# Sums of w_out by accumulating transfers: four whole ones, the last two issued behind the low words of w_in

## The chip, the cores and the metric

The kernel runs on one core of one Trainium2 chip. The metric is the device time of an execution in microseconds, as the median of several runs.

## What is computed

The reference first runs a chunked state-space block over `x`, `a`, `B` and `C` (batch 4, 8 heads, 768 tokens, 32 channels a head, 16 states), then brings its output into the shape 3072 tokens by 256 channels, and runs a two-layer block on it:

```
x = attn_out.transpose(0, 2, 1, 3).reshape(3072, 256)
h = x @ w_in                                  # 256 x 2048
g = where(h > 0, h, exp(min(h, 0)) - 1)       # ELU
out = g @ w_out                               # 2048 x 256
```

All inputs and the output are float32 (the two weights come in 64 bits and are brought to float32 on the chip).

## The kernel before

The tokens are cut into 12 blocks of 256 (`BLK`), numbered `n`. For each block the scan (scores, decays, states) makes its rows `y`, the first layer makes 2048 hidden values in tiles of 128 features, and the second layer multiplies them with `w_out`. The order of all instructions on all engines is written out by hand; there is no planner. An engine works off its own instructions in this order, and waits for semaphores where another engine or a transfer has to be done first. GpSimd and ScalarE also issue transfers, and these stand in the same order as their other work.

The first blocks take both layers directly (`l1`, `l2`). From block 2 on, blocks go in pairs:

- First layer, `l1_words(n, m)`: activations and weights are split into a high and a low word, and three passes of products fill two PSUM tiles, `ps_h` and `ps_w`. Then ScalarE scales `ps_w` into `e` (L796), VectorE joins it to `ps_h` (L799), ScalarE makes the exponential (L805, L806 in `begin_end`), and VectorE writes the hidden values `g` (L813 in `end_words`). The weights' words come from `words_of_w(p)` (ScalarE L737 and VectorE L738) and `low_of_w(p)` (two GpSimd subtractions, by `sub`, L848), for eight pieces `p` of `w_in`.
- Second layer, `second(n)`: a seven-product scheme over two blocks and two halves of `w_out`. It needs four blocks of `w_out`, called `a11, a12, a21, a22` here (`a_out[0]`, `[1]`, `[2]`, `[3]`), and four sums of them: `s3 = a11 - a21`, `s2 = a22 - s3`, `s4 = a12 - s2`, and `s1 = a21 + a22`. `s2, s3, s4` are tiles of their own (`s_out[0]`, `[1]`, `[2]`); `s1` is written over `a21`, so `a_out[2]` holds it from then on. Products are taken in the order r = 0 to 6 with the weights `(a11, a12, s1, s2, s3, a22, s4)`, first for four of the eight feature pairs `i` (half 0), then for the other four. GpSimd supplies differences of the hidden values: `sum_t1`, `sum_t2`, and the subtractions behind r = 0 and r = 1.

The sums of `w_out` are made by two helpers. `less` is a ScalarE instruction (L711) that writes the negative of one block into a sum's tile. `plus` (L715) is a transfer, issued by GpSimd, that adds one block to what stands at its destination. A whole block is 8 pieces of 128 by 128 for all partitions, 512 KB.

Around the change the order is this. The loop over `j` from 8 to 15 (`i = j - 8`) runs the first layer of block pair 2 with `l1_words(2, j)`, and puts in between the words of `w_in`, the second layer of block 1 by `l2(1, 0)` to `l2(1, 7)`, which reads all of the unchanged `w_out` (its last two steps at `i == 7`), and the scan of blocks 4 and 5. Behind the loop come `end_words()`, the low words of pieces 1 and 2, transfers, the words of piece 3, `decay(6, 0)`, the low words of piece 3, `sum_t2(2, 0)` (four subtractions) and one more subtraction on GpSimd. Then the loop over `n = 4, 6, 8, 10` begins: sixteen steps `k`, each an `l1_words(n, k)` of 6 products and some steps of `second(n - 2)`, four products for r = 0 in the first step and three steps or so a step after that. `turn_step` puts the scan's next operands in between, among them `mask_heads` (L465, the tile `ctm`) on VectorE. The text calls the way from the `j` loop into `n = 4` the first border.

In `second`, the products at r = 2 are the first that read `s1`, and those at r = 6 the first that read `s4`. The tile for r = 0, 2, 4, 6 of half 0 comes from a pool with one buffer, so r = 2 begins only when r = 0's tile was copied away to `p_sum` (L919, ScalarE).

Of the kernel before, what the change touches and what calls it, by code (L numbers as in the profile page):

```python
# [14 lines left out]
ALU = mybir.AluOpType  # L15
# [17 lines left out]
def kernel(  # L33
# [27 lines left out]
    nc = tc.nc  # L61
# [30 lines left out]
    for k in range(4):  # L92
        (nc.scalar if k % 2 else nc.sync).dma_start(
            out=la0[BH * k:BH * (k + 1)],
            in_=a.rearrange("b h (c s) -> (b h) c s", s=P)[:, 0:2, :])
# [25 lines left out]
    def load_bc(n, c_queue=nc.sync, us=(0, 1)):  # L121
        b, g = place(n)
        if "bc" not in st.setdefault(n, {}):
            st[n]["bc"] = raw.tile([P, 2, 2, NH, N], F32, tag="bc", name="bc", bufs=2)
        if n > 3:
            for k in range(2):
                load_squares(n, k)
            return
        for u in us:
            sl = slice((2 * g + u) * P, (2 * g + u + 1) * P)  # L130
            for k, src in enumerate((B,) if n == 1 else (B, C)):
                (nc.sync, c_queue)[k].dma_start(
                    out=st[n]["bc"][:, k, u], in_=src[b, :, sl, :].rearrange("h s n -> s h n"))

    def load_b(n):
        b, g = place(n)
        st.setdefault(n, {})["b"] = raw.tile([P, 2, NH, N], F32, tag="b", name="b_tok", bufs=2)
        for u in range(2):
            sl = slice((2 * g + u) * P, (2 * g + u + 1) * P)
            nc.sync.dma_start(  # L140
                out=st[n]["b"][:, u], in_=B[b, :, sl, :].rearrange("h s n -> s h n"))
# [141 lines left out]
    for v in range(2):  # L283
        nc.gpsimd.affine_select(
            out=low16[Q * v:Q * v + Q], in_=low16[Q * v:Q * v + Q], pattern=[[1, Q]],
# [5 lines left out]
        out=hmask, in_=hmask, pattern=[[-N, NH]], compare_op=ALU.is_ge, fill=0.0,  # L291
        base=0, channel_multiplier=1)
    nc.gpsimd.affine_select(
        out=hmask, in_=hmask, pattern=[[N, NH]], compare_op=ALU.is_ge, fill=0.0,
# [8 lines left out]
        out=minus, in0=ident, scalar1=-1.0, scalar2=None, op0=ALU.mult)  # L303
# [102 lines left out]
    def scaled(n, eng):  # L406

        s = st[n]
        s["sc"] = sc = s["b"] if n > 3 else raw.tile(
            [P, 2, NH, N], F32, tag="b", name="sc", bufs=2)  # L410
        factor = eb0[:, :, NH * n:NH * (n + 1)] if n < 2 else eb[:, :, rows_of(n)]
        eng.tensor_tensor(
            out=sc, in0=s["b"] if n > 3 else s["bc"][:, 0],
            in1=factor.unsqueeze(3).to_broadcast([P, 2, NH, N]), op=ALU.mult)
# [54 lines left out]
    def turn_part(n, part):  # L469
        if part < 2:  # L470
            turn_square(n, 1 - part)
        elif part == 2:
            mask_heads(n)
        else:
            turn_exp(n)
# [233 lines left out]
    def less(out, in_):  # L709

        nc.scalar.activation(out, in_, ACT.Copy, scale=-1.0)  # L711

    def plus(out, in_, rows=slice(None)):

        nc.gpsimd.dma_start(out=out[:, rows], in_=in_[:, rows], accum_op=ALU.add)  # L715

    def weight_sums():
        return [conv.tile([P, MC // 2, P], F32, tag="w64", name="w_sum", bufs=W_AHEAD)
# [3 lines left out]
    a_out = [w_parts[:, k, r] for r in range(2) for k in range(2)]  # L722
    s_out = []
# [8 lines left out]
    def words_of_w(i):  # L732

        w = pieces[i][0]
        k_words[i] = conv.tile(
            [P, 2, KC, CW], F32R, tag="w64", name="w_words", bufs=W_AHEAD)
        nc.scalar.activation(k_words[i][:, 0], w, ACT.Copy, scale=NEAR)  # L737
        nc.vector.scalar_tensor_tensor(  # L738
            out=k_words[i][:, 1], in0=k_words[i][:, 0].bitcast(F32), scalar=1.0 / WORD - 1.0,
            in1=w, op0=ALU.mult, op1=ALU.add)  # L740

    def low_of_w(i):

        w0 = conv.tile([P, KC, CW], F32R, tag="w_in", name="w0", bufs=DF // CW + 1)
        for k in range(KC):
            sub(w0[:, k], pieces[i][0][:, k], k_words[i][:, 0, k].bitcast(F32))
        k_words[i] = k_words[i], w0
# [30 lines left out]
    def l1_words(n, m, between=None):  # L778

        cols = slice(m % 2 * P, (m % 2 + 1) * P)  # L780
        w, w0 = k_words[m // 2]
        w1, both_w, w0 = w[:, 0, :, cols], w[:, 1, :, cols], w0[:, :, cols]
        y1, y0, both_y = y_words[n]
        high, both = psum([P, 2 * BLK], "ps_h"), psum([P, 2 * BLK], "ps_w")
        passes = [(high, w1, y1), (high, w0, y0), (both, both_w, both_y)]
        for ps, lhs, rhs in passes if m == (8 if n == 2 else 0) or m == 15 else passes[2:] + passes[:2]:
            for k in range(KC):
                nc.tensor.matmul(  # L788
                    out=ps, lhsT=lhs[:, k], rhs=rhs[:, k], start=k == 0 and lhs is not w0,
                    stop=k == KC - 1 and lhs is not w1)  # L790
        if between:
            words_of_y(between)
            if between == 4:
                both_of_y(4)
        e = ffn.tile([P, 2 * BLK], F32, tag="e", name="e", bufs=2)
        nc.scalar.activation(e, both, ACT.Copy, scale=WORD)  # L796
        if late:
            end_words()
        nc.vector.scalar_tensor_tensor(  # L799
            out=high, in0=high, scalar=WORD - 1.0, in1=e, op0=ALU.mult, op1=ALU.add)  # L800
        late.append((n, m, high, e))

    def begin_end():
        high, e = late[-1][2:]
        nc.scalar.activation(e, high, ACT.Relu, scale=-1.0)  # L805
        nc.scalar.activation(e, e, ACT.Exp, scale=-1.0)  # L806
# [12 lines left out]
    def row_of(n):  # L819
        b, g = place(n)  # L820
        return b * S + g * BLK
# [3 lines left out]
    def l2(n, j, half=None):  # L825


        if j == 0 and half != 1:
            o_of[n] = p_o.tile([P, 2, DM], F32, tag="o", name="ps_o")
        for m in (2 * j, 2 * j + 1) if half is None else (2 * j + half,):  # L830
            for ts in range(2):
                nc.tensor.matmul(  # L832
                    out=o_of[n][:, ts], lhsT=g_of[n, j][:, m % 2, ts * P:(ts + 1) * P],
                    rhs=w_out[:, m], start=(m == 0 and ts == 0), stop=(m == MC - 1),
                    skip_group_check=True)
        if j == MC // 2 - 1 and half != 0:
            ob = ffn.tile([P, 2, DM], F32, tag="tmp", name="ob", bufs=1)
            nc.scalar.copy(out=ob, in_=o_of.pop(n))
            r0 = row_of(n)
            nc.sync.dma_start(  # L840
                out=out[r0:r0 + BLK, :].rearrange("(t p) e -> p t e", p=P), in_=ob)
# [5 lines left out]
    def sub(out, in0, in1):  # L847
        nc.gpsimd.tensor_tensor(out=out, in0=in0, in1=in1, op=ALU.subtract)  # L848
# [291 lines left out]
    def weigh_two(m, q):  # L1140
        weigh(m, q)
        weigh(m + 1, q)
# [29 lines left out]
    for j in range(2 * DIRECT):  # L1172
        n, i = 2 + j // DIRECT, j % DIRECT
# [53 lines left out]
    for j in range(8, 16):  # L1227
        i = j - 8
        l1_words(2, j, between=4 if i == 7 else None)
        for p in ((), (6,), (), (7,), (0,), (1,), (2,), ())[i]:  # L1230
            words_of_w(p)
        for p in ((), (), (6,), (7,), (0,), (), (), ())[i]:
            low_of_w(p)
        if i == 7:
            l2(1, 6)
            l2(1, 7)
        begin_end()
        if i == 0:
            turn_part(5, 2)
            scaled(4, nc.gpsimd)  # L1240
            scaled(5, nc.gpsimd)
        if i < 2:
            load_bc(i + 6)
            l2(1, i)
        if i == 2:
            l2(1, 2, half=0)
            scores(4, 5)
            sums(4, 5)
            for q in range(4):
                weigh_two(4, q)  # L1250
            l2(1, 2, half=1)
            states(4)
            states(5)
            turn_part(4, 3)
            turn_part(5, 3)
            for to in (6, 7):
                load_b(to)
                spread_cum(to)
        if i == 3:
            l2(1, 3)  # L1260
        if i == 4:
            y = across(4, 5)
            inside(y, 4, 5, ts=(0,))
            l2(1, 4)
        if i == 5:
            l2(1, 5, half=0)
            inside(y, 4, 5, ts=(1,))
            l2(1, 5, half=1)
        if i in (0, 1, 3, 4):
            sum_t1(2, (0, 1, 3, 4).index(i))  # L1270
        if i in (4, 6):
            turn_part(6, i // 2 - 2)
        if i == 2:
            less(s_out[0], s_out[1])
            plus(s_out[0], a_out[3])
        if i == 5:
            plus(a_out[2], a_out[3], slice(0, 4))
    end_words()
    less(s_out[2], s_out[0])
    for p in (1, 2):  # L1280
        low_of_w(p)
    plus(s_out[2], a_out[1])
    plus(a_out[2], a_out[3], slice(4, 8))
    words_of_w(3)
    decay(6, 0)
    low_of_w(3)
# [102 lines left out]
```

## Time and profile before

| | |
|---|---|
| median of 3 runs | 355.28 us (354.91 to 355.96) |
| profiled execution | 354.39 us |
| its span, first to last instruction | 352.7 us |
| mean granted TensorE clock | 0.99 |
| PE busy | 342.7 us, 97% of the span |
| DVE (VectorE) busy | 258.6 us, 73% |
| ACT (ScalarE) busy | 238.2 us, 68% |
| POOL (GpSimd) busy | 214.9 us, 61% |
| accumulating transfers | 5 issues on GpSimd: 3 of 512 KB, 2 of 256 KB |

In the views, PE is TensorE's products and PEld its weight loads. A row of a timeline has the start and the length in us from the start of the span, the engine, the line of the kernel, the operation, what it writes and reads with the shape, and how many were merged into the row; a bracket at the end is idle time of that engine just before, and what ended it. A row of the stretches has the stretch, its length, the busy time of PE, PEld, DVE, ACT and POOL with their counts, the granted TensorE clock as a share of full speed, the busy share of the DMA engines and GB/s. GpSimd's rows can overlap, because an instruction is recorded from when it is taken up.

### The profile page before, as it was taken

The numbers are of one execution on the slowest core, as the hardware profiler recorded it, in microseconds if no ns is written. First come the engines' busy times: TensorE is split into PE (matmuls) and PEld (weight loads), VectorE is DVE, ScalarE is ACT, GpSimd is POOL, SyncE is SP. The second block draws the span as 40 slices with busy tenths as digits, with TensorE's granted clock in tenths as the row PEclk, the third lists the DMA queues.
The fourth block names the chain that finished last, engine by engine and source line by source line (L and its number), as shares of the span: only waits on it lengthen the run. The fifth ranks groups of instructions, "written<-read, shape, count | busy, mean of one in ns | idle before, by whom it ended". The sixth has DMA issues, their size and how long they took to land.

```text
span 352.7 us, 9862 instructions
## 1 busy us (share of the span) xinstructions
PE 342.7 (97%) x3878; PEld 299.9 (85%) x3878; DVE 258.6 (73%) x504; ACT 238.2 (68%) x541; POOL 214.9 (61%) x321
## 2 busy tenths in 40 slices
PE   8999999999999869999999999999999999999996
PEld 5669888888787759988989988899988999999996
DVE  3898979979889677784978685878685757565232
ACT  5789988798766858837599737599646666655000
POOL 5654564569896695975176964086954074455760
PEclk9999999999999978999999999999999999999999
DMA  8977988473693940052150062140000100001001
GB/s 144 253 200 175 309 196 209 89 127 64 102 187 47 171 62 30 4 92 78 52 113 30 2 113 58 61 74 3 0 2 4 62 0 3 0 0 46 17 1 60
DMA packets 76902, 28.58 MB, mean 81 GB/s; under 512 B 57848, under 2 KB 71736, under 8 KB 76856
## 3 DMA queue, kind: packets, MB, share of 16 engines
q1 hardware_dynamic: 70360, 25.60, 31.1%
q0 software_dynamic: 4176, 2.10, 5.4%
q8 instruction: 30, 0.49, 0.6%
q10 hardware_dynamic: 2320, 0.26, 0.5%
q14 instruction: 16, 0.13, 0.1%
HBM read 22.51 MB, written 3.34 MB: 73 GB/s over the span
## 4 chain that ended last, share of the span: by engine, by line
PE 82%; DVE 7%; ACT 3%; issue 3%; SPq 2%; DMA 2%; POOL 0%; DVEq 0%; POOLq 0%; ACTq 0%
PE ps_o L907 34%; PE ps_h L788 17%; PE ps_h L671 11%; PE ps_w L788 8%; PE ps_o L832 5%; PE ps_y L638 2%; PE ps_g L545 2%; DMA w<-in_moe_w_in_dram 2%; PE ps_y L620 1%; DVE ps_h L799 1%; PE ps_st L575 1%; DVE w_words L738 1%; DVE M L554 1%; DVE g L813 1%; DVE ctm L465 1%
## 5 line engine op out<-in xcount | busy, mean ns | idle before, releaser
L907 PEld LDWEIGHTS ps_o<-w_out,g 128*128 128x128 f32 x640 | 78.6, 191 | 4.5 <-ACT p_sum L919 1.1
L907 PE MATMUL ps_o<-w_out,g 128*128 128x128 f32 x640 | 80.3, 275 | 0.9 <-ACT p_sum L919 0.9
L805 ACT ACTIVATE e<-ps_h 128x512 f32<-128x512 f32 x72 | 43.0, 598 | 55.9 <-DVE ps_h L799 55.9
L813 DVE SCALAR_TENSOR_TENSOR g<-e,ps_h 128x512 f32<-128x512 f32 x72 | 49.3, 685 | 34.4 <-ACT e L806 34.0
L848 POOL TENSOR_TENSOR g<-g 128x256 f32<-128x256 f32 x36 | 29.2, 811 | 57.9 <-DVE g L813 57.7
L799 DVE SCALAR_TENSOR_TENSOR ps_h<-ps_h,e 128x512 f32<-128x512 f32 x72 | 50.0, 694 | 13.0 <-ACT e L796 10.4
L788 PE MATMUL ps_w<-y_both,w_words 128*128 128x512 f32 x144 | 52.0, 440 | 1.5 <-DVE g L813 1.4
L796 ACT ACTIVATE e<-ps_w 128x512 f32<-128x512 f32 x72 | 42.3, 587 | 14.2 <-PE ps_w L788 14.1
L788 PE MATMUL ps_h<-y,w_words 128*128 128x512 f32 x144 | 47.0, 408 | 1.7 <-ACT e L796 1.7
L806 ACT ACTIVATE e<-e 128x512 f32<-128x512 f32 x72 | 45.5, 632 | 2.3
L671 PE MATMUL ps_h<-yT,w_in 128*128 128x256 f32 (+1 forms) x208 | 45.2, 368 | 1.4 <-POOL w_in L252 1.3
L788 PE MATMUL ps_h<-y,w 128*128 128x512 f32 x144 | 45.1, 394 | 0.0
L671 PEld LDWEIGHTS ps_h<-yT,w_in 128*128 128x128 f32 x208 | 36.3, 190 | 7.5 <-POOL w_in L252 2.8
L525 ACT ACTIVATE L<-L,ncum 128x64 f32<-128x64 f32 x160 | 42.2, 336 | 0.2
L907 PE MATMUL ps_o<-w_sum,g 128*128 128x128 f32 x304 | 38.3, 275 | 0.0
L530 POOL TENSOR_SCALAR_AFFINE_SELECT L<-L 64x512 f32<-64x512 f32 x40 | 31.2, 781 | 11.1 <-ACT L L525 8.9
L907 PEld LDWEIGHTS ps_o<-w_sum,g 128*128 128x128 f32 x304 | 37.1, 192 | 1.0
L788 PEld LDWEIGHTS ps_h<-y,w_words 128*128 128x128 f32 x144 | 26.8, 192 | 7.8 <-ACT e L796 2.1
L788 PEld LDWEIGHTS ps_h<-y,w 128*128 128x128 f32 x144 | 27.4, 191 | 6.6 <-POOL w L848 0.2
L848 POOL TENSOR_TENSOR g<-t,g 128x256 f32<-128x256 f32 x40 | 28.0, 733 | 5.8 <-PE ps_o L907 5.7
L832 PE MATMUL ps_o<-w_out,g 128*128 128x256 f32 x128 | 31.0, 384 | 0.0
L848 POOL TENSOR_TENSOR t<-g 128x256 f32<-128x256 f32 x40 | 29.8, 865 | 0.2
(131 smaller groups left out, 546.2 us busy)
## 6 DMA issues: line engine op xcount, KB each, us to landing
L<-flat SPq DMA_DIRECT2D x20, 256.0 KB
w<-in_moe_w_out_dram SPq DMA_DIRECT2D x8, 512.0 KB
w<-in_moe_w_in_dram SPq DMA_DIRECT2D x7, 512.0 KB
xr<-in_x_dram SPq DMA_DIRECT2D x24, 128.0 KB
out_dram<-c_sum SPq DMA_DIRECT2D x9, 256.0 KB
bc<-in_B_dram SPq DMA_DIRECT2D x24, 64.0 KB
w_sum<-w_out POOLq DMA_DIRECT2D x3, 512.0 KB, 8.7
bc<-in_C_dram SPq DMA_DIRECT2D x22, 64.0 KB
```

The source lines that it names most:

```text
L525: nc.scalar.activation(L[:, h, u], L[:, h, u], ACT.Exp, bias=ncum[:, u, row:row + 1])
L530: nc.gpsimd.affine_select(out=part, in_=part, pattern=[[0, 4], [0, 2], [1, Q]], compare_op=ALU.is_ge, fill=0.0, base=0, channel_multiplier=-1)
L671: nc.tensor.matmul(out=ps[:, j, toks], lhsT=w_in[i][:, k, j * P:(j + 1) * P], rhs=yT[n // 2][:, k, n % 2].rearrange("p u i -> p (u i)")[:, ...
L788: nc.tensor.matmul(out=ps, lhsT=lhs[:, k], rhs=rhs[:, k], start=k == 0 and lhs is not w0, stop=k == KC - 1 and lhs is not w1)
L796: nc.scalar.activation(e, both, ACT.Copy, scale=WORD)
L799: nc.vector.scalar_tensor_tensor(out=high, in0=high, scalar=WORD - 1.0, in1=e, op0=ALU.mult, op1=ALU.add)
L805: nc.scalar.activation(e, high, ACT.Relu, scale=-1.0)
L806: nc.scalar.activation(e, e, ACT.Exp, scale=-1.0)
L813: nc.vector.scalar_tensor_tensor(out=g_of[n, m].rearrange("p b i -> p (b i)"), in0=e, scalar=1.0, in1=h, op0=ALU.subtract, op1=ALU.max)
L832: nc.tensor.matmul(out=o_of[n][:, ts], lhsT=g_of[n, j][:, m % 2, ts * P:(ts + 1) * P], rhs=w_out[:, m], start=(m == 0 and ts == 0), stop=( ...
L848: nc.gpsimd.tensor_tensor(out=out, in0=in0, in1=in1, op=ALU.subtract)
L907: nc.tensor.matmul(out=ps[:, ts], lhsT=b[:, ts * P:(ts + 1) * P], rhs=a[:, i], start=(i == chunk[0] and ts == 0), stop=(i == chunk[-1]), s ...
```

## The change

`plus` loses its argument for a part of the rows. The transfer of the first four pieces of `s1` at `i == 5` is taken out, and the one of the other four, behind the low words, becomes a transfer of all eight. It is now issued ahead of the transfer for `s4`, and not behind it. The `less` for `s4` moves from behind `end_words()` to `i == 7` inside the loop, ahead of `begin_end()`.

```diff
-    def plus(out, in_, rows=slice(None)):
+    def plus(out, in_):
 
-        nc.gpsimd.dma_start(out=out[:, rows], in_=in_[:, rows], accum_op=ALU.add)
+        nc.gpsimd.dma_start(out=out, in_=in_, accum_op=ALU.add)
...
         if i == 7:
             l2(1, 6)
             l2(1, 7)
+            less(s_out[2], s_out[0])
         begin_end()
...
         if i == 2:
             less(s_out[0], s_out[1])
             plus(s_out[0], a_out[3])
-        if i == 5:
-            plus(a_out[2], a_out[3], slice(0, 4))
     end_words()
-    less(s_out[2], s_out[0])
     for p in (1, 2):
         low_of_w(p)
+    plus(a_out[2], a_out[3])
     plus(s_out[2], a_out[1])
-    plus(a_out[2], a_out[3], slice(4, 8))
     words_of_w(3)
     decay(6, 0)
     low_of_w(3)
```

## The prediction

> **What bounds the kernel now.** I read the page first, then TensorE's timeline around the changed lines, then the timelines of VectorE, GpSimd and ScalarE for the same microseconds, and last the landings of the transfers.
>
> All times below are of this one execution, 354.39 us with what lies around its span. That is 0.89 us under the median of the three runs, 355.28, so I work out a difference and take it off the median. About 0.3% (1.1 us) is what a measurement of this kernel can tell from no change.
>
> TensorE is the engine that the rest must feed. Its timeline at the first border (the step from `l2(1, 7)` into the loop `n == 4`):
>
> ```profile
> 109.25 3.61 PE L832 MATMUL ps_o<-w_out,g 128*128 128x256 f32 x16
> ...
> 120.09 1.05 PE L907 MATMUL ps_o<-w_out,g 128*128 128x128 f32 x8
> 122.06 0.71 PE L907 MATMUL ps_o<-w_out,g 128*128 128x128 f32 x4 [0.92 <-ACT p_sum L919]
> ...
> 123.99 1.50 PE L907 MATMUL ps_o<-w_out,g 128*128 128x128 f32 x12
> 126.91 0.73 PE L788 MATMUL ps_w<-y_both,w_words 128*128 128x512 f32 x2 [1.42 <-DVE g L813]
> 129.30 1.22 PE L788 MATMUL ps_h<-y,w_words 128*128 128x512 f32 x2 [1.65 <-ACT e L796]
> ...
> 136.27 1.06 PE L907 MATMUL ps_o<-w_sum,g 128*128 128x128 f32 x8
> ```
>
> The brackets are idle time: 0.92, 1.42 and 1.65 us, 4.0 us together. The two long ones have a second price, the granted clock (the last column but two):
>
> ```profile
> 128.00:130.00 2.00, 0.70 (x2) 0.61 (x3) 1.22 (x4) 1.97 (x7) 2.00 (x4) 0.61 0.14 30
> 130.00:134.00 4.00, 4.00 (x17) 3.71 (x16) 2.51 (x6) 3.53 (x9) 4.00 (x7) 0.50 0.00 0
> ```
>
> TensorE is busy for 4.00 us at half clock and 0.70 at 0.61, so some 2.0 + 0.3 = 2.3 us more are lost there. Who held it up is on VectorE:
>
> ```profile
> 105.79 3.03 DVE L738 SCALAR_TENSOR_TENSOR w_words<-w_words,w_in 128x512 fp32r<-128x512 f32 x1
> ...
> 118.24 0.69 DVE L738 SCALAR_TENSOR_TENSOR w_words<-w_words,w_in 128x512 fp32r<-128x512 f32 x1 [0.78 <-ACT w_words L737]
> ...
> 120.29 5.97 DVE L465 TENSOR_TENSOR ctm<-bct,hmask 128x512 f32<-128x512 f32 x1
> ```
>
> and beside it GpSimd:
>
> ```profile
> 105.53 1.96 POOL L715 DMA_DIRECT2D w_out<-w_out  x1
> 106.37 4.99 POOL L848 TENSOR_TENSOR w<-w_in,w_words 128x256 fp32r<-128x256 f32 x4
> 117.99 1.56 POOL L715 DMA_DIRECT2D w_sum<-w_out  x1 [6.63 <-ACT w_sum L711]
> 118.93 1.94 POOL L715 DMA_DIRECT2D w_out<-w_out  x1
> 119.72 2.58 POOL L848 TENSOR_TENSOR w<-w_in,w_words 128x256 fp32r<-128x256 f32 x2
> 121.09 3.93 POOL L848 TENSOR_TENSOR t<-g 128x256 f32<-128x256 f32 x4
> 123.85 1.85 POOL L848 TENSOR_TENSOR g<-g 128x256 f32<-128x256 f32 x1
> ```
>
> The two long VectorE instructions read both operands from SBUF, and each stands in front of a GpSimd queue in which subtractions follow directly behind an accumulating transfer. How odd they are shows in the rows of their lines (min/median/max in ns):
>
> ```profile
> L738 DVE SCALAR_TENSOR_TENSOR w_words<-w_words,w_in x8: 692/900/3033, 78.5 to 118.2; 128x512 fp32r<-128x512 f32 x8
> L465 DVE TENSOR_TENSOR ctm<-bct,hmask x9: 674/906/5971, 18.9 to 241.5; 128x512 f32<-128x512 f32 x9
> L715 POOL DMA_DIRECT2D w_sum<-w_out x3: 1565/1565/1769, 84.4 to 118.0; - x3
> ```
> ```profile
> 76.84 1.75 DVE L763 SCALAR_TENSOR_TENSOR y<-y,yT 128x512 fp32r<-128x512 f32 x1
> ```
>
> L465 lost 5.97 - 0.67 = 5.3 us, L738 3.03 - 0.69 = 2.3. The longest row of the same kind outside the transfers is L763's: two operands of the same size in SBUF, at 76.84, before the first accumulating transfer at 84.4. It loses 1.75 - 0.69 = 1.06. And L738 at 118.24 ran in its shortest time inside the transfer issued at 117.99. So I read it thus: not the transfer alone holds VectorE, but a string of GpSimd work queued right behind it. The string at 119.72 is seven subtractions long; the ctm ends as the last of them does (123.85 + 1.85 = 125.70, and 125.70 + its own 0.67 is near 126.26).
>
> The Trainium skill, page "SBUF — State Buffer", section "Who interferes with whom", says that a VectorE instruction with two SBUF inputs contends with a GpSimd instruction that reads SBUF, that the loser waits for that whole instruction, and that descriptor writing should not hold a tensor_tensor. By this rule one wait is one instruction; the 5.97 us row is seven of them, and there the measurement decides. But the rule blames the subtractions, which this change keeps; that is the first rival below.
>
> **The change part by part.**
>
> *The transfer at i == 5 goes.* `plus(a_out[2], a_out[3], slice(0, 4))` at 105.53 is removed. L738 at 105.79 then costs 0.69 to about 1.8 (L763's worst) in place of 3.03, and GpSimd's first low words come up to 1 us sooner. TensorE is without idle rows from here to 121.14, so I cost this at nothing: it brings a few tenths to VectorE's words of y, and what TensorE gains by it is swallowed at `s1` below.
>
> *`less(s_out[2], s_out[0])` moves up by one step.*
>
> ```profile
> 112.89 0.59 ACT L838 COPY ob<-ps_o 128x512 f32<-128x512 f32 x1 [0.57 <-PE ps_o L832]
> 115.48 0.60 ACT L805 ACTIVATE e<-ps_h 128x512 f32<-128x512 f32 x1 [2.00 <-DVE ps_h L799]
> ...
> 116.65 1.04 ACT L711 ACTIVATE w_sum<-w_sum 128x1024 f32<-128x1024 f32 x1
> 117.60 0.61 ACT L737 ACTIVATE w_words<-w_in 128x512 fp32r<-128x512 f32 x1
> ...
> 121.66 0.35 ACT L919 COPY p_sum<-ps_o 128x256 f32<-128x256 f32 x1
> ```
>
> It takes 1.04 us and lands between L838 (ends 113.48) and L805 (115.48), where ScalarE idles 2.00 us. Its input is the sum of the second full transfer, which the timeline has issued at 98.18; by the slowest landing of a full one below, 9.6, it is down by 107.8. So the move is free there, and L737, the decays, L796 and L919 behind it come about 1.0 us earlier: the copy to p_sum ends near 121.0 and not 122.0, and the 0.92 us wait of TensorE at 122.06 loses its cause. If VectorE became faster by over 0.9 us before 114.8, the cover would be short by as much.
>
> *The two transfers behind the low words.* `plus(a_out[2], a_out[3])`, now all eight rows, waits for the last `l2(1, 7)` product (109.25 + 3.61 = 112.86), since that still reads the old w_out; GpSimd idles there (6.63 us in the row of 117.99), and nothing queued behind it is ready. It issues at about 113.0. `plus(s_out[2], a_out[1])` follows when the `less` is done, 113.5 + 1.04, at about 114.8, and its issue is over by 116.4. The next GpSimd work, `low_of_w(3)`, waits for L737, whose row ends at 118.21, now about 117.2. So the string begins with no transfer in front of it, and by the reading above ctm costs 0.67, at the most 1.06 more. Is that soon enough? It is asked for 1.04 earlier, at 119.25, and ends between 119.9 and 121.0 (119.25 + 0.67, and 1.06 more). TensorE's high product of the fifth step stood 129.30 - 126.26 = 3.04 us behind ctm's end, and would be wanted at 125.9 if TensorE ran on from 125.49; so ctm may end as late as 122.9 for nothing. All three idles go.
>
> *What comes next: the first use of `s1`.* The half transfer that landed long before is gone. `second(2)` reads `a_out[2]` at r == 2, the x4 row at 122.06, so the whole sum must be down by then. Landings, first of the 512 KB transfers into w_sum, then of all five:
>
> ```profile
> DMA to landing us min/median/max: 8.1/8.7/9.6
> ```
> ```profile
> DMA to landing us min/median/max: 4.8/8.7/10.1
> ```
>
> 113.0 + 8.7 = 121.7. TensorE reaches the place at 121.14 (120.09 + 1.05). So a new wait of about 0.6 us, from 0 (8.1) to 1.5 (9.6), or 2.0 by the slowest landing of all, 10.1. I take the median, because the three full transfers agree within 0.9 each way. The Trainium skill, page "DMA: Bandwidth & Descriptors", section "Anatomy of one DMA — SWDGE (gpsimd) path", gives 2.0 us plus bytes over 436 GB/s for a transfer that GpSimd issues; as an estimate that is 3.2 us here, `s1` would never be waited for, and the gain would be 7.3. No landing of this size in the trace is under 8.1, so the trace decides.
>
> **The sum.** A step of the steady loop takes
>
> ```profile
> 182.62 1.34 PE ps_o L907 x12
> ...
> 185.34 1.34 PE ps_o L907 x12
> ```
>
> 2.72 us. From the end of the fourth step (123.99 + 1.50 = 125.49) two more would end at 130.93; the second of them ends at 137.33 now (136.27 + 1.06). That is 6.40 us, with r == 2 still beginning at 122.06. With `s1` at 121.7 it begins about 0.3 earlier: 6.7. I keep 0.3 back for contention of single instructions: 6.4. Behind this border TensorE's rows run at that 2.72 pitch to the end, so it stays saved: 354.39 - 6.4 = 348.0, and 355.28 - 6.4 = 348.9 as a median. Bounds of this case: `s1` at 8.1 gives 6.40 + 0.92 = 7.3, 348.0; at 10.1 (123.1) it gives 5.3, 350.0; with the spread of the runs 347.5 to 350.5.
>
> **The rivals.**
>
> *The string holds VectorE without a transfer ahead of it.* For it: seven subtractions are still queued together, and they end as ctm does. Against it: L763's 1.06 is the worst loss with no transfer near. If ctm still takes 5.97 it ends 1.04 earlier than now, and everything behind it too: 354.2. A shorter hold lies between this and 348.9; only past 122.9 does it cost anything. The same comes about if the change does not do what it says, because the `less` slips behind and the second transfer again meets `low_of_w(3)`.
>
> *`s1` lands too late, slower.* The place is the x4 row at 122.06. The two transfers at 117.99 and 118.93 (512 and 256 KB) were all down 118.93 + 10.1 - 117.99 = 11.0 us after the first issue, 2.9 after the first landed. If the two whole ones share the engines packet by packet, both land 14 to 15 us after 113.0, at 127 to 128: r == 2 is 5.0 to 5.9 late, the idle of some 6 us costs the clock as now, 2.3, and 6.4 - 5.0 - 2.3 or 6.4 - 5.9 - 2.3 is a loss of 0.9 to 1.8: 356.2 to 357.1. It decides from 126.2 on (a landing after 13.1 us). Against it: the first of that pair landed after at most 9.6, with the second right behind it.
>
> **How the numbers follow.** The forecast has 0.76, the hold 0.12 (half of it short enough to be over 0.3% faster, half within), the late `s1` and whatever else makes it slower 0.12. So faster 0.82, same 0.06, slower 0.12. The forecast's own range leaves some of its 0.76 outside, so the range goes on towards the shorter holds: 347.4 to 353.2.
>
> **What would show it.** Right: four L715 rows on GpSimd, the last two near 113 and 115; L711's third row ahead of L805; no L465 or L738 row over 1.8 us; the granted clock at 1.00 through 128 to 138; TensorE at r == 2 near 121.8, released by a transfer. Wrong: a ctm of 3 us or more with the first transfer gone; a TensorE idle of over 2 us in front of r == 2 named after the DMA; a VectorE row at 112 to 114 (L763, L773) held by the first transfer's issue for over 1 us, with TensorE waiting for y_both.

## The result

The changed kernel takes 349.52 us (median of 6 runs, 348.64 to 350.63) against 355.25 us of the kernel before (6 runs): a ratio of 0.984, 95% interval 0.982 to 0.986, or 5.7 us less. The forecast was 348.9 in a range of 347.4 to 353.2. The profiled execution has a span of 347.4 us against 352.7.

TensorE's timeline at the first border, changed kernel:

```profile
109.96 3.61 PE L832 MATMUL ps_o<-w_out,g 128*128 128x256 f32 x16
...
120.57 1.05 PE L907 MATMUL ps_o<-w_out,g 128*128 128x128 f32 x8
122.42 0.68 PE L907 MATMUL ps_o<-w_out,g 128*128 128x128 f32 x4 [0.80 <-DMA w_out<-w_out]
...
124.33 1.50 PE L907 MATMUL ps_o<-w_out,g 128*128 128x128 f32 x12
125.58 0.71 PE L788 MATMUL ps_w<-y_both,w_words 128*128 128x512 f32 x2
126.13 0.63 PE L788 MATMUL ps_h<-y,w_words 128*128 128x512 f32 x2
...
130.22 1.06 PE L907 MATMUL ps_o<-w_sum,g 128*128 128x128 f32 x8
```

This execution comes to the L832 row 0.71 us later than the one before did (109.96 against 109.25), from the start of the kernel on, so the border is measured from there: the end of the x8 row stands 130.22 + 1.06 - 109.96 = 21.3 us behind it, where it stood 136.27 + 1.06 - 109.25 = 28.1. The border has lost 6.8 us. The two idles of 1.42 and 1.65 us are gone, and the one at r == 2 has another releaser: the transfer of `s1`. The granted clock (last column but two) stays at 1.00:

```profile
128.00:130.00 2.00, 2.00 (x13) 1.74 (x13) 1.49 (x5) 1.93 (x5) 2.00 (x4) 1.00 0.24 73
130.00:134.00 4.00, 4.00 (x31) 3.74 (x30) 2.67 (x6) 3.53 (x11) 3.85 (x7) 1.00 0.25 75
```

VectorE, then GpSimd, both of the changed kernel:

```profile
106.52 2.38 DVE L738 SCALAR_TENSOR_TENSOR w_words<-w_words,w_in 128x512 fp32r<-128x512 f32 x1
...
119.81 1.25 DVE L465 TENSOR_TENSOR ctm<-bct,hmask 128x512 f32<-128x512 f32 x1
```
```profile
104.91 1.37 POOL L861 TENSOR_TENSOR g<-g 128x256 f32<-128x256 f32 x1
105.59 1.37 POOL L848 TENSOR_TENSOR g<-g 128x256 f32<-128x256 f32 x1
106.53 1.81 POOL L848 TENSOR_TENSOR w<-w_in,w_words 128x256 fp32r<-128x256 f32 x2
...
113.01 1.56 POOL L715 DMA_DIRECT2D w_out<-w_out  x1 [0.67 <-PE ps_o L832]
115.45 1.54 POOL L715 DMA_DIRECT2D w_sum<-w_out  x1 [0.88 <-DVE g L813]
117.86 1.95 POOL L848 TENSOR_TENSOR w<-w_in,w_words 128x256 fp32r<-128x256 f32 x2 [0.87 <-issue]
119.78 3.24 POOL L848 TENSOR_TENSOR t<-g 128x256 f32<-128x256 f32 x4
122.97 0.74 POOL L848 TENSOR_TENSOR g<-g 128x256 f32<-128x256 f32 x1
```

The same seven subtractions stand behind 117.86, but 0.87 us of idle time lie between the transfer and them, and ctm takes 1.25 us where it took 5.97. A finer sign is in the groups of four: t<-g takes 3.24 us for four, 0.81 each on the mean, and the next row starts at 122.97, before 119.78 + 3.24 = 123.02 by 0.05. Before, the t<-g row ended at 121.09 + 3.93 = 125.02 and the next one was taken up at 123.85, 1.17 us earlier. GpSimd's records overlapped all through that string. The text calls such records, each taken up before the one ahead of it has ended, a backlog.

### The profile page after: what moved, and what is told of

Read it like the earlier page. It is cut to its first block, busy times and chain, and to the rows that moved or that the text cites. A ratio compares the mean times of both kernels' runs of the same rounds, so it can differ in the third digit from the quotient of the medians.

```text
span 347.4 us, 9861 instructions
## 1 busy us (share of the span) xinstructions
PE 340.3 (98%) x3878; PEld 298.2 (86%) x3878; DVE 253.7 (73%) x504; ACT 237.8 (68%) x541; POOL 214.2 (62%) x320
## 4 chain that ended last, share of the span: by engine, by line
PE 78%; DMA 5%; ACT 5%; DVE 5%; SPq 3%; issue 2%; POOL 1%; DVEq 0%; POOLq 0%; ACTq 0%
PE ps_o L907 32%; PE ps_h L788 15%; PE ps_h L671 11%; PE ps_w L788 8%; PE ps_o L832 5%; DMA w_out<-w_out 3%; PE ps_y L638 2%; DMA w<-in_moe_w_in_dram 2%; DVE ps_h L799 1%; PE ps_g L545 1%; PE ps_y L620 1%; ACT e L806 1%; ACT e L805 1%; SPq L148 1%; PE ps_st L575 1%
## 5 line engine op out<-in xcount | busy, mean ns | idle before, releaser
L848 POOL TENSOR_TENSOR g<-g 128x256 f32<-128x256 f32 x36 | 28.4, 789 | 56.4 <-DVE g L813 56.1
L788 PE MATMUL ps_w<-y_both,w_words 128*128 128x512 f32 x144 | 51.0, 434 | 0.0
L788 PE MATMUL ps_h<-y,w_words 128*128 128x512 f32 x144 | 46.2, 402 | 0.0
L530 POOL TENSOR_SCALAR_AFFINE_SELECT L<-L 64x512 f32<-64x512 f32 x40 | 29.6, 741 | 10.0 <-ACT L L525 8.6
L832 PE MATMUL ps_o<-w_out,g 128*128 128x256 f32 x128 | 31.0, 384 | 0.0
L848 POOL TENSOR_TENSOR t<-g 128x256 f32<-128x256 f32 x40 | 29.0, 757 | 0.2
```

The costliest lines, as they stand in the source:

```text
L530: nc.gpsimd.affine_select(out=part, in_=part, pattern=[[0, 4], [0, 2], [1, Q]], compare_op=ALU.is_ge, fill=0.0, base=0, channel_multiplier=-1)
L788: nc.tensor.matmul(out=ps, lhsT=lhs[:, k], rhs=rhs[:, k], start=k == 0 and lhs is not w0, stop=k == KC - 1 and lhs is not w1)
L832: nc.tensor.matmul(out=o_of[n][:, ts], lhsT=g_of[n, j][:, m % 2, ts * P:(ts + 1) * P], rhs=w_out[:, m], start=(m == 0 and ts == 0), stop=( ...
```

## The experiments

Three explanations stood against each other. **A**: a transfer issued right in front of a string of GpSimd subtractions makes the string hold VectorE's ctm. **B**: fewer transfers cost less. **C**: ScalarE gains by the `less` moved out of its way. All ratios are to the kernel before, timed on the same chip beside the run (354.46 us for the less alone, the less put back, the shorter string and s1 in halves; 354.69 us for the other three). The changed kernel again, beside those three:

> The changed kernel again, beside the others on this chip: 349 to 350, ratio 0.982 to 0.986, ctm 1.2 to 1.3 us, a wait of 0.5 to 1.5 us at r == 2.

Measured: 348.96 us, ratio 0.984 (0.981 to 0.986).

**The less alone.** To the kernel before, only this:

```diff
             l2(1, 7)
+            less(s_out[2], s_out[0])
...
-    less(s_out[2], s_out[0])
```

> The kernel before with one part of the change alone: the less for s4 moved to i == 7; still five transfers, the half at i == 5 and the half behind s4 as before. Theory A (the gain is that no transfer stands directly in front of the string of GpSimd subtractions): the two last transfers issue near 114.8 and 115.8 and are over by 117.7, just as the low words of piece 3 come up (117.2), so ctm takes 1 to 2 us instead of 5.97; the first half of s1 is down early, so r == 2 waits for ScalarE's copy only, and the time is 348.7 to 349.7. Theory B (fewer transfers make the gain): five transfers as before, so 354 to 355.5, ctm 4 us or more.

Measured: 349.18 us, ratio 0.984 (0.982 to 0.987), and ctm

```profile
120.06 1.25 DVE L465 TENSOR_TENSOR ctm<-bct,hmask 128x512 f32<-128x512 f32 x1
```

Five transfers, and the whole gain. B falls: neither the number of transfers nor the whole instead of the halves matters. The removal of the transfer at i == 5 brings nothing that can be told. GpSimd's rows narrow A as well:

```profile
116.38 1.94 POOL L715 DMA_DIRECT2D w_out<-w_out  x1
118.12 1.94 POOL L848 TENSOR_TENSOR w<-w_in,w_words 128x256 fp32r<-128x256 f32 x2
120.03 3.25 POOL L848 TENSOR_TENSOR t<-g 128x256 f32<-128x256 f32 x4
```

A transfer still stands right in front of the string, and the first subtraction is taken up 0.20 us before its issue is over (116.38 + 1.94 = 118.32), yet ctm is not held. Within the string the records overlap by no more than 0.03 us here (118.12 + 1.94 = 120.06, and the next row starts at 120.03).

**The changed kernel with the less put back.**

```diff
             l2(1, 7)
-            less(s_out[2], s_out[0])
         begin_end()
...
     end_words()
+    less(s_out[2], s_out[0])
     for p in (1, 2):
```

> The changed kernel with the less for s4 put back behind end_words: four transfers, s1 whole and first, s4 last. Theory A: s1 still issues at 113, but s4 waits for the less until 118 and stands right in front of the low words of piece 3, so ctm is held again for 4 to 6 us and TensorE's clock drops: 353.5 to 355.3. Theory B: four transfers as in the changed kernel, so 349.5 to 350.5 (1 us for the less on ScalarE at most), ctm under 2 us.

Measured: 352.82 us, ratio 0.995 (0.992 to 0.997). Its GpSimd and VectorE rows:

```profile
118.40 1.54 POOL L715 DMA_DIRECT2D w_sum<-w_out  x1 [3.88 <-ACT w_sum L711]
119.31 2.08 POOL L848 TENSOR_TENSOR w<-w_in,w_words 128x256 fp32r<-128x256 f32 x2
```
```profile
120.70 4.66 DVE L465 TENSOR_TENSOR ctm<-bct,hmask 128x512 f32<-128x512 f32 x1
```

The transfer is back in front of the string, the subtraction is taken up at 119.31 while the transfer's issue runs to 119.94, and ctm is held again. The time came out 0.7 us under the range expected. The clock, which I expected to drop, stayed at 1.00 behind the wait, so the 2.3 us that the prediction read off the clock before are not lost here:

```profile
130.00:134.00 4.00, 4.00 (x29) 3.56 (x28) 2.97 (x6) 3.56 (x10) 4.00 (x7) 1.00 0.06 17
```

ctm's 4.66 is 1.3 us less than the 5.97 of before. That one transfer delays the string by less than two is the likely reason, and was not tried by itself.

**The less left late, the transfers put behind the string.** This parts A from C. The kernel before with

```diff
-    plus(s_out[2], a_out[1])
-    plus(a_out[2], a_out[3], slice(4, 8))
     words_of_w(3)
...
     sub(g_of[2, 14][:, 1], g_of[2, 14][:, 1], g_of[2, 14][:, 0])
+    plus(s_out[2], a_out[1])
+    plus(a_out[2], a_out[3], slice(4, 8))
```

> The kernel before with its two last transfers moved behind the seven subtractions (behind the one on g[2, 14]); five transfers, the less on ScalarE where it was. Theory A (backlog behind a transfer): nothing stands in front of the subtractions, they start with GpSimd idle, ctm takes 0.7 to 1.8 us and the gain of the change comes without it: 348.7 to 350, although ScalarE still has the less in its way. Theory C (the less moved off ScalarE's way makes the gain): 354 or more. If it is the string of subtractions itself that holds ctm: ctm 2.5 to 3.5 us and 350 to 352.

Measured: 350.00 us, ratio 0.986 (0.984 to 0.989), ctm 1.18 us:

```profile
118.61 1.90 POOL L848 TENSOR_TENSOR w<-w_in,w_words 128x256 fp32r<-128x256 f32 x2 [6.99 <-ACT w_words L737]
...
124.36 1.54 POOL L715 DMA_DIRECT2D w_sum<-w_out  x1
```

Most of the gain comes without touching ScalarE. The 1.0 us between this and the changed kernel beside it (348.96) is what is left for C and for whatever else differs; TensorE waits 0.90 us for the copy to p_sum here, as it did before.

**A shorter string.** The kernel before with the four subtractions of `sum_t2` ahead of the transfers:

```diff
+    sum_t2(2, 0)
     plus(s_out[2], a_out[1])
     plus(a_out[2], a_out[3], slice(4, 8))
...
     low_of_w(3)
-    sum_t2(2, 0)
```

> The kernel before with sum_t2(2, 0), four subtractions, moved ahead of the two last transfers, so that three subtractions instead of seven stand behind them; nothing else. If the whole string behind a transfer holds VectorE (theory A): ctm ends some 2.7 us sooner, 2.5 to 3.8 us instead of 5.97, and the time is 350 to 352. If it is the transfers' own issue that holds it, whatever stands behind: ctm 5.5 to 6.2, 354.8 to 355.8.

Measured: 353.67 us, ratio 0.997 (0.996 to 0.999); VectorE's ctm, then GpSimd's string:

```profile
122.81 3.27 DVE L465 TENSOR_TENSOR ctm<-bct,hmask 128x512 f32<-128x512 f32 x1
```
```profile
121.45 1.94 POOL L715 DMA_DIRECT2D w_out<-w_out  x1
122.24 2.61 POOL L848 TENSOR_TENSOR w<-w_in,w_words 128x256 fp32r<-128x256 f32 x2
123.64 1.88 POOL L848 TENSOR_TENSOR g<-g 128x256 f32<-128x256 f32 x1
```

The hold shrinks as the string does, and its end is again the end of the last subtraction (125.52, and 125.52 + 0.67 is near 126.08, where ctm ends). The time I expected was missed by 1.7 us: the four moved subtractions now run beside VectorE's words of y, which read two operands from SBUF as well (two L763 take 2.17 us and two L773 2.35, before 1.29 and 1.28). TensorE waits for those, and behind the waits its clock is at 0.50 from 118 to 120 us:

```profile
114.65 0.47 PE L788 MATMUL ps_h<-y,w 128*128 128x512 f32 x1 [0.53 <-DVE y L763]
115.69 0.50 PE L788 MATMUL ps_w<-y_both,w_words 128*128 128x512 f32 x1 [0.57 <-DVE y_both L773]
116.83 0.50 PE L788 MATMUL ps_w<-y_both,w_words 128*128 128x512 f32 x1 [0.63 <-DVE y_both L773]
```

**A gap between transfer and string.** The kernel with the less put back (352.82), and with both decays ahead of the subtractions:

```diff
     decay(6, 0)
+    decay(6, 1)
     low_of_w(3)
...
-            if n == 4 and k == 0:
-                decay(6, 1)
```

> The kernel of e2_less_late (ctm 4.66 us, s4's transfer right in front of the seven subtractions), with decay(6, 1) pulled in front of them: GpSimd's two selections for it wait for ScalarE until about 120.2, some 0.2 us after the transfer's issue is over, and only then the subtractions follow. Same transfers, same subtractions, one wait between. If the backlog (instructions taken up while the transfer's issue is still running) is what holds VectorE: ctm 0.7 to 1.8 us, and the time falls from 352.8 to 349.8 to 351.5, less what the eight exponentials put ahead on ScalarE cost (up to 1 us). If any string behind a transfer holds it: ctm 4 us or more, 353 to 354.5.

Measured: 350.63 us, ratio 0.988 (0.986 to 0.991). GpSimd, then VectorE:

```profile
118.12 1.54 POOL L715 DMA_DIRECT2D w_sum<-w_out  x1 [3.84 <-ACT w_sum L711]
120.32 1.39 POOL L530 TENSOR_SCALAR_AFFINE_SELECT L<-L 64x512 f32<-64x512 f32 x2 [0.66 <-ACT L L525]
121.80 1.73 POOL L848 TENSOR_TENSOR w<-w_in,w_words 128x256 fp32r<-128x256 f32 x2
```
```profile
121.37 0.88 DVE L465 TENSOR_TENSOR ctm<-bct,hmask 128x512 f32<-128x512 f32 x1
```

The same transfer in front of the same subtractions, with 0.66 us of idle time between: 0.88 us instead of 4.66. TensorE waits 1.78 us for the copy to p_sum, since ScalarE does the exponentials first; even so 2.2 us are gained on the kernel it was made from. So the transfer's presence alone does not hold ctm. But more than the gap has changed: ctm is asked for at 121.37, while the selections run, before the first subtraction at 121.80. That subtractions without a backlog do not hold it is shown by the run with the transfers behind the string and by the changed kernel, where ctm starts in the middle of the string.

**The two transfers swapped.**

```diff
-    plus(a_out[2], a_out[3])
     plus(s_out[2], a_out[1])
+    plus(a_out[2], a_out[3])
```

> The changed kernel with its two last transfers swapped: s4 first, which waits for the less (about 115.2), then s1 at about 116.1. Both are out of the way of the low words of piece 3 only by halves: the second is over near 118. My theory: s1 lands 9.5 to 11 us after 116.1, at 125.6 to 127.1, so TensorE waits 4 to 5.5 us at r == 2 instead of 0.8, the clock may drop behind that; ctm 1.2 to 3 us. The time is 3.5 to 6.5 us over the changed kernel, 353 to 356. If the transfers of one queue share the engines evenly, s1 lands little later than now and the time is within 1 us of the changed kernel.

Measured: 354.77 us, ratio 1.001 (0.999 to 1.003). The whole gain is gone, with the same four transfers; `s1` is issued at 115.44 and not at 113.01, which is 6.42 us behind the start of the L832 row and not 3.05. GpSimd, VectorE, TensorE and a stretch of it:

```profile
115.44 2.20 POOL L715 DMA_DIRECT2D w_out<-w_out  x1
116.91 2.19 POOL L848 TENSOR_TENSOR w<-w_in,w_words 128x256 fp32r<-128x256 f32 x2
118.81 3.00 POOL L848 TENSOR_TENSOR t<-g 128x256 f32<-128x256 f32 x4
```
```profile
118.84 4.81 DVE L465 TENSOR_TENSOR ctm<-bct,hmask 128x512 f32<-128x512 f32 x1
```
```profile
125.68 1.19 PE L907 MATMUL ps_o<-w_out,g 128*128 128x128 f32 x4 [5.01 <-DMA w_out<-w_out]
```
```profile
126.00:128.00 2.00, 2.00 (x8) 1.71 (x8) 1.62 (x3) 2.00 (x7) 2.00 (x4) 0.50 0.36 86
```

`s1` lands 10.1 us after its issue, TensorE waits 5.01 us for it, and runs at half clock behind that. This is the place of the prediction's slower rival and nearly its idle time, reached by another road: `s1` is issued late here, where the rival had it land slowly. Its time, 356.2 to 357.1, is not reached. For ctm I expected 1.2 to 3 us, and that was wrong. The first subtraction is taken up 0.73 us before the issue ends (115.44 + 2.20 = 117.64), within the string the overlap is only 0.29 (116.91 + 2.19 = 119.10, the next row at 118.81), and ctm is held for 4.81 us all the same. How the two costs share the loss was not parted.

**s1 in halves.** The changed kernel with `plus(a_out[2], a_out[3], slice(0, 4))` and `slice(4, 8)` in place of the whole transfer:

> The changed kernel with s1's transfer cut into its first and second four pieces, issued at the same place one behind the other (five transfers). If the 0.80 us wait at r == 2 is the landing of the whole s1: the first half lands about 5 us after 113, the wait goes, r == 2 begins at the copy to p_sum, 0.7 to 0.9 us sooner, and the time is 0.3 to 0.8 us under the changed kernel, 348.7 to 349.2. Theory B: one transfer more costs, 349.5 or more. If what is gained there is given back where TensorE waits in the scan's sums of the same pair: 349.5, no change.

Measured: 348.75 us, ratio 0.983 (0.981 to 0.986). The wait at r == 2 is gone (no idle row there), but a new one stands later:

```profile
137.29 1.94 PE L907 MATMUL ps_o<-w_sum,g 128*128 128x128 f32 x15 [0.38 <-ACT c_sum L944]
```

The interval is all but that of the changed kernel run again (0.981 to 0.986), so the 0.80 us of `s1` are worth nothing that can be told here, though 348.75 lies in the range that I had given for a gain. The traces show where they go: the first L638 row (a product of the scan) behind the border starts 47.10 us behind the L832 row (156.66 - 109.56), in the changed kernel 47.06 (157.02 - 109.96).

## Why the prediction was right

- **The stall and its end.** Right: ctm 1.25 us in the changed kernel, within the 0.67 to 1.73 given; both long idles and the loss of clock went with it. The condition, no transfer in front of the string, is not quite what I put down: with the less alone a transfer is in front, and ctm is not held. What goes with a hold is an overlap of GpSimd's records in the string: some 1.2 us before and in the shortened string, 0.7 with the less put back, 0.29 with the swap (all held), 0.05 in the changed kernel and 0.03 with the less alone (not held). That the overlap is not enough by itself is shown in the last section.
- **The removed transfer at i == 5.** The price of nothing for TensorE held; the size on VectorE was wrong. L738 takes 2.38 us, over my upper bound of 1.8, with no transfer near it; one of my signs, no L738 row over 1.8 us, did not come. GpSimd's rows at 104.91 and 105.59 last 1.37 us for work that takes 0.74 at 122.97: GpSimd had not been idle since the transfer at 98.91, and its backlog was, as I read it, still in the queue. My bound came from L763, where GpSimd's records overlap by no more than 0.04 us; that was the wrong neighbour.
- **The less.** Right. Its row lies in ScalarE's idle time, with 0.79 us of it left, and the copy to p_sum comes early enough not to be waited for (it ends at 121.17 + 0.35 = 121.52, and TensorE comes to r == 2 at 121.62):

```profile
114.09 1.06 ACT L711 ACTIVATE w_sum<-w_sum 128x1024 f32<-128x1024 f32 x1
115.94 0.60 ACT L805 ACTIVATE e<-ps_h 128x512 f32<-128x512 f32 x1 [0.79 <-DVE ps_h L799]
```

- **The new wait for s1.** Forecast 0.6 us (0 to 2.0), measured 0.80. The landing was 9.3 us instead of 8.7, the issue came sooner against the L832 row than I had it (3.05 us behind its start, not 3.75): it starts at 113.01, while the row of these products ends at 113.57. The experiment with the halves shows that the wait is cheap, since the same time is lost later, by the first L638 row.

```profile
DMA to landing us min/median/max: 9.3/9.3/9.3
```

- **The sum.** The border gave 6.8 us; the working had 6.7, and 6.4 after what I kept back. That it "stays saved" was a little off. TensorE gives 0.7 us back at the scan's sums, where it now is ahead of VectorE; the changed kernel, then the one before:

```profile
144.59 0.32 PE L575 MATMUL ps_st<-xr,b_tok 64*32 64x64 f32 x8
145.32 0.84 PE L575 MATMUL ps_st<-xr,b_tok 64*32 64x64 f32 x56 [0.41 <-DVE c_sum L885]
```
```profile
150.59 0.86 PE L575 MATMUL ps_st<-xr,b_tok 64*32 64x64 f32 x64
```

  From the start of the first L575 row to the end of the last it takes 1.57 us, before 0.86: 0.7 more. So 6.8 - 0.7 = 6.1 remain, and 5.7 is what the medians show; the last 0.4 are within the spread of the runs. That the 0.3 I kept back takes up part of this is luck: it stood for contention of single instructions, and the loss came as a wait in the scan. The clock's price before was read too small: it was at 0.84 from 134 to 138 us as well, with TensorE busy all the time, some 0.6 us more than the 2.3. The sum does not hang on it, since it took whole rows.
- **The rivals.** The string of subtractions did not hold VectorE where its records hardly overlapped. The late `s1` did not happen here, but the swapped order shows that a late `s1` does cost idle time and the clock at that place, and that with the order of two transfer issues the whole gain comes or goes.

## What to carry to other kernels

When a two-operand VectorE instruction is several times as long as its siblings, look at GpSimd's rows beside it: records that overlap are a backlog, and in these runs a transfer that GpSimd issued stood in front of it. Put such a transfer where GpSimd next has to wait for something anyway, or behind the work; in these runs the number of transfers mattered less than what was queued directly behind them. A wait that appears in the place of one removed is worth attacking only if the time is not lost again behind it: here 0.8 us taken away came back as other waits.

## What I had not expected

An overlap of 0.29 us between GpSimd's records went with a hold of 4.81 us, a little more than the 4.66 us behind one transfer with an overlap of 0.7. Such a hold of ctm lasts about as long as the string, not one instruction: it ends near the last subtraction before, with the less put back and in the shorter string, and 0.5 us later with the swap (121.56 + 0.93 + 0.67 = 123.16; ctm ends at 123.65). Where the records hardly overlap, in the changed kernel and three others whose ctm starts in the string, it takes 1.18 to 1.26 us, so it loses 0.5 to 0.6 us, less than the 0.7 us of one subtraction.

But an overlap is not always a hold. In the kernel before, two L738 rows fall into a string with overlaps of 1.15 us (99.14 + 1.84 = 100.98 against 99.83) and 1.10 us (101.65 + 1.87 = 103.52 against 102.42), right behind a transfer, and take 0.92 and 0.82 us. GpSimd, then VectorE:

```profile
98.18 1.56 POOL L715 DMA_DIRECT2D w_sum<-w_out  x1
99.14 1.84 POOL L848 TENSOR_TENSOR g<-g 128x256 f32<-128x256 f32 x1
99.83 2.51 POOL L848 TENSOR_TENSOR w<-w_in,w_words 128x256 fp32r<-128x256 f32 x2
101.65 1.87 POOL L861 TENSOR_TENSOR g<-g 128x256 f32<-128x256 f32 x1
102.42 2.46 POOL L848 TENSOR_TENSOR w<-w_in,w_words 128x256 fp32r<-128x256 f32 x2
```
```profile
99.49 0.92 DVE L738 SCALAR_TENSOR_TENSOR w_words<-w_words,w_in 128x512 fp32r<-128x512 f32 x1
...
102.11 0.82 DVE L738 SCALAR_TENSOR_TENSOR w_words<-w_words,w_in 128x512 fp32r<-128x512 f32 x1
```

So every row of L465 and L738 over 1.8 us in these traces lies among overlapping records, but not every row among overlapping records is long. What else a hold takes is open.
